# Copies of row sums moved from VectorE to GpSimd, and seven products in place of eight for one more block of tokens, in a fused attention and MLP kernel

## The chip, the cores and the metric

The kernel runs on one core of a Trainium2 chip. The core has five engines that each work through their own queue in order and meet by semaphores: TensorE (PE, matrix products), VectorE (DVE), ScalarE (ACT), GpSimd (POOL) and SyncE (SP, which here only issues DMAs). The metric is the device time of one execution in microseconds (us); lower is better.

## The reference

Attention over chunks of 64 keys, 8 batches, 8 heads, 576 rows, head size 64, and then a two-layer MLP with exact GELU on the 4608 tokens of 512 numbers that come out:

```
scores = (q_c @ k_c^T) / 8               # 64 x 64 blocks, one per batch, head and chunk
attn   = exp(scores - max); attn /= sum(attn) + 1e-9
x      = (attn @ v_c), heads side by side  # 4608 x 512
h      = x @ w_in                          # 512 x 2048
out    = (0.5 * h * (1 + erf(h / sqrt 2))) @ w_out
```

Inputs and outputs are float32. The kernel multiplies in bf16 and leaves out the subtraction of the maximum.

## The kernel before, in words

**Tiling.** The tokens are cut into nine tiles of 512, index t = 0 to 8. Tiles 0 to 7 hold the first eight chunks of one batch each, tile 8 the last chunk of all batches. A loop over t (L934) does for each index one *mm1* (x times w_in, GELU by ACT, result h) and one *mm2* (h times w_out, stored). Into the mm2 of index t, and into the mm1 of index t+1, the attention of a later tile is woven, so that PE always has something to do. The order of all engines is written out by hand: lists called `order`, `e1` (mm1) and `e2` (mm2) hold functions by step, and the place at which a function is called is the place of its instructions in each engine's queue. Nothing is reordered afterwards.

**mm1 with sixteen row blocks ("dense").** `mm1_slot` (L448) takes one block of 128 of the 2048 rows of h: four matmuls of 128x512, then one GELU (L455) out of one of three PSUM banks of the pool ps_mm. Indices in `DENSE` (L459) do this sixteen times.

**mm1 with seven products.** The other indices replace row blocks 0 to 3 by a 2x2 scheme with seven products instead of eight (`seven_rows` L508, `mm1_seven` L549): steps p1 to p7 are products of four 128x256 matmuls each (L523), built from sums of quarters of x (`x_sums` L502, four VectorE subtractions at L506) and of w_in. Three PSUM banks a, b, d collect them. ACT copies p1, p5 and u2 out (L527), VectorE adds a bank to such a copy (L530, steps c11, c12 and c22+), ACT applies GELU (L534). Step p3 is added into bank a, and so has to wait until the VectorE step c22+ has read bank a. Twelve row blocks remain dense.

**mm2 with seven products** (`mm2_seven` L604, matmuls at L664) needs sums of h. `g_sum` forms them on VectorE: sum 3 (L589, one instruction of 2048 columns), and sums 1, 2 and 4 in two halves each (L602, 1024 columns). The third product of mm2 reads both halves of sum 2. VectorE adds banks to copies at L631 and `store_block` lets SP issue the stores.

**The attention of tile n = t+1 from index 4 on.** In the mm2 of index t: scores of tile n+1 on PE (`quad_S` L231, 64 matmuls at L237, in four PSUM banks), exponentials on ACT (L244), and partial row sums on VectorE (`quad_part` L248: a transpose L254 and a reduction L257, four times). In the mm1 of index t+1 follows `quad_total` (L260): the sums lie in quarters of 32 partitions, and eight VectorE copies of 32 partitions by 32 numbers (L268, a quarter to its neighbour quarter) bring the missing half of each sum across; then for each half a reduction (L272), a reciprocal (L274), copies across (L279), and `quad_rc` (L281, L283), which spreads the reciprocals over columns, one of four tiles rc at a time. At the head of the next mm2 PE forms the value products (`quad_av`, 64 matmuls at L317, in four banks), and VectorE multiplies each bank by its rc into the next x (`quad_x` L321, L324). The four banks of `quad_S` in the same mm2 are the banks of `quad_av`, so PE's second half of the scores waits until the third and fourth of these multiplications are done.

**Loads.** `bring_qk` and `load_v_rows` let SP issue loads of q, k and v, and GpSimd casts what has landed to bf16 (L164, L212). In the body of index t stand, in this order, `flip_qk` of t+2 (two DMA transposes on SP), and then `next_loads`: q and k of t+3, v of t+2, with GpSimd's casts. SP's queue is in order too: the stores of index t-1 stand before these.

Of the kernel before, what the change touches and what calls it, by code (L numbers as in the profile page):

```python
# [11 lines left out]
def kernel(  # L12
# [20 lines left out]
    G = H // 2  # L33
# [5 lines left out]
    NT = B + 1  # L39
# [21 lines left out]
    QD = P // G  # L61
# [40 lines left out]
    tiles = [dict() for _ in range(NT)]  # L102
# [145 lines left out]
    def quad_part(t, g2, c):  # L248

        st = tiles[t]  # L250
        if c == 1:
# [5 lines left out]
        nc.vector.tensor_reduce(st["part", g2][:, c, :, :, 0], pt[:].rearrange("p n e u -> p n u e"),  # L257
                                axis=mybir.AxisListType.X, op=mybir.AluOpType.add)

    def quad_total(t, halves=range(2)):  # L260

        part = [tiles[t]["part", g2] for g2 in range(2)]
        if 0 in halves:
            tiles[t]["across"] = [work.tile([P, NB], f32, tag="across", name="across", bufs=2) for _ in range(2)]
            for g2 in range(2):
                for s in range(G):
                    o = s ^ 1
                    DV(part[g2][QD * s:QD * (s + 1), :, :, :, 1], part[g2][QD * o:QD * (o + 1), :, :, :, 0])  # L268
        across = tiles[t]["across"]
        for g2 in halves:  # L270
            total, rb = (work.tile([P, 2, NB], f32, tag=nm, name=nm, bufs=2) for nm in ("total", "rb"))
            nc.vector.tensor_reduce(total[:], part[g2][:].rearrange("p c n u s -> p c (n u) s"),  # L272
                                    axis=mybir.AxisListType.X, op=mybir.AluOpType.add)
            nc.vector.reciprocal(rb[:], total[:])  # L274
            tiles[t]["rb", g2] = rb[:, 0], across[g2][:]
            if g2 == 0:
                quad_rc(t, 0, 0)
            for r in range(2):
                DV(across[g2][CH * r:CH * (r + 1)], rb[CH * (1 - r):CH * (2 - r), 1])  # L279
# [176 lines left out]

    NQ = 4
    T0 = 3
    DENSE = (0, 1, T0 + 1)  # L459

    HF = FF // 2
    HD = d_model // 2
# [86 lines left out]
    def mm1_seven(t, hooks):  # L549

        tiles[t]["h"] = hpool.tile([P, FF, MT], bf16, tag="h", name="h")
        does = seven_rows(t, 0, {"a": AT, "b": AT, "d": AT}, AC)
        if t == NT - 1:
            sums = stage_tile()[:].bitcast(bf16).rearrange("p (i ks f) -> p i ks f", ks=2, f=HD)
            w_in_sum.append([sums[:, i] for i in range(4)])
            does["w"] = lambda: w_in_sums(1)
            more = seven_rows(t, 1, {"a": TP, "b": TP, "d": AT}, DV)
            does.update((step + "'", do) for step, do in more.items())
            order = ("p1", "p2", "p5", "c11", "w", 8, "p6", 9, "p4", "p7", "c12", "c22+", 10, "c22", "p1'", "p2'", "p3", 11,
                     "c11'", "p5'", 12, "p6'", 13, "p4'", "p7'", "c12'", "c22+'", 14, "c22'", "p3'", 15, "g0", "s3")  # L560
        elif t > T0:
            order = ("p1", "p2", "p5", "c11", "t0", 4, "p6", 5, 6, "p4", "p7", "c12", "c22+", "t1", 7, "c22", 8, 9, "p3",
                     10, "s3", 11, 12, 13, "g0", 14, 15)
        elif t == T0:
            order = ("x", "p1", "p2", 4, "p5", "c11", 5, "p6", 6, "p4", "p7", "c12", "c22+", 7, "c22", 8, "p3",
                     9, 10, "s3", 11, 12, 13, "g0", 14, 15)
        else:
            order = ("x", 4, 5, 6, "p1", "p2", 7, "p5", "c11", 8, "p6", 9, "p4", "p7", "c12", "c22+", 10, "c22", 11, "p3",
                     12, "s3", 13, "g0", 14, 15)
        for step in order:  # L570
            if step in does:
                does[step]()
                continue
            for u in hooks.get(step, ()):
                u()
            if not isinstance(step, str):
                mm1_slot(t, step)
# [230 lines left out]
    with tc.manual_schedule():  # L808
# [116 lines left out]
        def flip_qk(t):  # L925
            for nm in "qk":
                flip(t, nm)
# [6 lines left out]
        for t in range(1, NT):  # L934
# [3 lines left out]
            if t == 1:  # L938
# [12 lines left out]
                load_v_rows(2, (1,))  # L951
                cast_v_rows(2, PO)
                bring_qk(3)
            elif t > T0 and n + 1 < NT:
                flip_qk(n + 1)
            def next_loads():
                if t + 3 < NT:
                    bring_qk(t + 3)
# [39 lines left out]
                    e2[12] = parts[0]  # L998
                    e2[13] = parts[1]
            elif n < NT:  # L1000
                rcs = [lambda m=m: quad_rc(n, m // 2, m % 2) for m in range(1, G)]
                if t not in DENSE:
                    e1["t0"] = [lambda: quad_total(n, (0,))]
                    e1["t1"] = [lambda: quad_total(n, (1,))] + rcs
                else:
                    e1[1] = [lambda: quad_total(n)]
                    e1[5] = rcs
                e2 = {0: [exp, lambda: quad_av(n, ALONE)] + xs[:2] + g[1][:2], 4: xs[2:] + g[1][2:],
                      6: [lambda: x_sums(n, (0, 1))], 10: [lambda: x_sums(n, (2, 3))], 11: [gelu]}
                if n + 1 < NT:  # L1010
                    for i, gs in enumerate(((0,), (1, 2), (3,))):
                        e2.setdefault(2 * i + 2, []).append(lambda gs=gs: k_by_chunk(n + 1, AC, gs))
                    e2[8] = [lambda: quad_S(n + 1, ALONE)] + parts[0]
                    e2[10] += parts[1]
# [29 lines left out]
```

## Time and profile before

| | us |
|---|---|
| median of 3 runs (275.07 to 275.83) | 275.24 |
| the profiled execution, its own time | 277.53 |
| span of the profile, first to last instruction | 275.7 |
| PE busy | 265.3 (96%) |
| VectorE busy | 206.9 (75%) |
| ACT busy | 192.2 (70%) |
| GpSimd busy | 85.4 (31%) |
| mean granted clock of PE | 0.993 |

Times in a profile count from the start of the span. In the timeline a row gives start, length, engine, line of the kernel, operation, tiles and how many instructions were merged; square brackets give idle time of the engine just before, and what ended it. In a table of stages each row gives a stretch of the span and how long each engine was busy in it. By the starts of PE's steps, mm1 of index 4 begins at 137.66 us, its mm2 at 151.47; mm1 of index 5 at 165.22, its mm2 at 178.63; mm1 of index 6 at 192.44, its mm2 at 205.86; mm1 of index 7 at 219.60.

### The profile page before, as it was taken

Reading aid. Unit: us, or ns where it says so; the run is one execution under the profiler, and the core shown is the slowest. Engines: PE = TensorE matmul, PEld = TensorE weight load, DVE = VectorE, ACT = ScalarE, POOL = GpSimd, SP = SyncE. Lnnn points to the kernel's source line nnn. Section 1 sums busy time; section 2 is a strip of 40 time slices with the busy share of each in tenths; the row PEclk is TensorE's granted clock in tenths of the full one; section 3 lists DMA queues with packets and bytes.
Section 4 is the critical chain, followed back from the end, with each engine's and each line's share of the span. In section 5 each row is a group of like instructions: output and inputs, shape, how many; then the busy total and the mean of one; then the engine's idle time right before and its main releaser. Section 6 shows DMA issues by size and latency. Waiting matters only on the chain.

```text
span 275.7 us, 7136 instructions
## 1 busy us (share of the span) xinstructions
PE 265.3 (96%) x2863; PEld 182.0 (66%) x2885; DVE 206.9 (75%) x377; ACT 192.2 (70%) x368; POOL 85.4 (31%) x142
## 2 busy tenths in 40 slices
PE   8798999999999999999999999999999999999993
PEld 6473455445886588558844886588558855886683
DVE  5779425896893988587899789878987898746831
ACT  2765666987867877877966967896689778358610
POOL 7779668401176226104405800032300200000000
PEclk9979999999999999999999999999999999999999
DMA  6999999769899899999599517999974120130014
GB/s 221 254 360 402 394 388 239 189 157 277 263 376 204 220 326 188 263 273 302 141 248 344 132 40 195 160 132 162 242 169 108 66 76 2 40 105 9 4 38 114
DMA packets 104737, 53.94 MB, mean 196 GB/s; under 512 B 72960, under 2 KB 101632, under 8 KB 104704
## 3 DMA queue, kind: packets, MB, share of 16 engines
q1 hardware_dynamic: 104400, 53.23, 73.9%
q8 instruction: 22, 0.36, 0.5%
q10 hardware_dynamic: 304, 0.26, 0.3%
q14 instruction: 11, 0.09, 0.1%
HBM read 36.70 MB, written 9.44 MB: 167 GB/s over the span
## 4 chain that ended last, share of the span: by engine, by line
PE 91%; ACT 4%; DVE 2%; issue 1%; ACTq 0%
PE y_ps L664 34%; PE h_ps L453 34%; PE hs_ps L523 8%; PE y_ps L736 3%; PE av_ps L317 2%; ACT k_bd L188 2%; PE h_ps L443 2%; PE s_ps L237 1%; PE y_ps L700 1%; PE rc_ps L395 1%; PE tp L175 1%; PE none L800 1%; PE warm L794 1%; ACT pT L336 1%; PE av_ps L408 1%
## 5 line engine op out<-in xcount | busy, mean ns | idle before, releaser
L453 PE MATMUL h_ps<-x,w_in_sb 128*128 128x512 bf16 x420 | 98.0, 379 | 2.2 <-DVE w_in_sb L780 1.3
L455 ACT ACTIVATE h<-h_ps 128x512 bf16<-128x512 f32 x109 | 64.3, 597 | 21.5 <-PE h_ps L453 21.2
L453 PEld LDWEIGHTS <-w_in_sb 128*128 128x128 bf16 x436 | 42.5, 98 | 46.2 <-DVE w_in_sb L780 1.8
L664 PEld LDWEIGHTS <-h 128*128 128x128 bf16 x384 | 37.0, 98 | 4.7
L164 POOL CAST q_nat<-arrival 128x512 bf16<-128x512 f32 x31 | 20.4, 698 | 62.2 <-DMA arrival<-in_q_dram 58.3
L212 POOL CAST v_nat<-arrival 128x1024 bf16<-128x1024 f32 x14 | 15.0, 1078 | 49.3 <-DMA arrival<-in_v_dram 49.3
L664 PE MATMUL y_ps<-v_bd,k_bd 128*128 128x256 bf16 x256 | 29.4, 273 | 0.1
L664 PE MATMUL y_ps<-w_out_sb,h 128*128 128x256 bf16 x256 | 29.3, 273 | 0.0
L664 PEld LDWEIGHTS <-k_bd 128*128 128x128 bf16 x256 | 24.8, 98 | 3.2 <-DVE w_out_sb L500 0.2
L631 DVE TENSOR_TENSOR kept<-y_ps,kept 128x512 f32<-128x512 f32 (+1 forms) x25 | 16.4, 656 | 12.3 <-PE y_ps L664 8.7
L806 ACT ACT_TABLE_LOAD x18 | 23.1, 1283 | 1.0 <-PEq L1028 0.7
L626 ACT COPY kept<-y_ps 128x512 f32<-128x512 f32 (+1 forms) x26 | 14.5, 556 | 12.3 <-PE y_ps L664 12.1
L164 POOL CAST k_nat<-arrival 128x512 bf16<-128x512 f32 x30 | 18.9, 666 | 11.8 <-DMA arrival<-in_v_dram 6.1
L530 DVE TENSOR_TENSOR arrival<-hs_ps,arrival 128x512 f32<-128x512 f32 x21 | 13.8, 685 | 11.2 <-PE hs_ps L523 7.2
L534 ACT ACTIVATE h<-arrival 128x512 bf16<-128x512 f32 x21 | 13.2, 628 | 6.6 <-DVE arrival L530 6.4
L664 PE MATMUL y_ps<-v_bd,s_sb 128*128 128x256 bf16 x128 | 15.3, 273 | 0.0
L664 PE MATMUL y_ps<-w_out_sb,s 128*128 128x256 bf16 x128 | 15.3, 273 | 0.0
L664 PE MATMUL y_ps<-v_bd,h 128*128 128x256 bf16 x128 | 15.3, 273 | 0.0
L244 ACT ACTIVATE pT<-s_ps 128x512 bf16<-128x512 f32 x28 | 14.4, 603 | 0.1
L602 DVE TENSOR_TENSOR k_bd<-h 128x1024 bf16<-128x1024 bf16 x16 | 11.1, 696 | 3.6 <-ACT h L455 3.4
L664 PEld LDWEIGHTS <-s 128*128 128x128 bf16 x128 | 12.4, 98 | 1.5
L636 ACT COPY y_sb<-y_ps 128x512 f32<-128x512 f32 x7 | 4.1, 586 | 13.2 <-PE y_ps L664 13.2
(130 smaller groups left out, 428.1 us busy)
## 6 DMA issues: line engine op xcount, KB each, us to landing
arrival<-in_v_dram SPq DMA_DIRECT2D x58, 128.0 KB, 4.0
arrival<-in_q_dram SPq DMA_DIRECT2D x7, 1024.0 KB, 6.5
arrival<-in_k_dram SPq DMA_DIRECT2D x6, 1024.0 KB, 9.3
out_dram<-kept SPq DMA_DIRECT2D x21, 256.0 KB, 2.7
arrival<-in_moe_w_out_dram SPq DMA_DIRECT2D x4, 1024.0 KB, 11.2
arrival<-in_moe_w_in_dram SPq DMA_DIRECT2D x6, 512.0 KB, 6.6
out_dram<-y_sb SPq DMA_DIRECT2D x11, 256.0 KB, 2.5
arrival<-in_k_dram SPq DMA_DIRECT2D x8, 256.0 KB, 5.3
```

Source lines behind the costliest of these rows:

```text
L164: copy(st[nm][:, g].rearrange("p j r d -> p r j d"), st[nm + "f"][:, 2 * g:2 * g + 2])
L212: copy(st["v"][:, r::2], st["vf"][:, r::2])
L244: nc.scalar.activation(pT[:].rearrange("p u (c j) -> p u c j", j=J), s_ps[g2][c][:].rearrange("p u (j c) -> p u c j", j=J), Act.Exp, scale ...
L453: nc.tensor.matmul(h_ps[:], w_in_sb[:, ks, f * P:(f + 1) * P], tiles[t]["x"][:, ks, :], start=(ks == 0), stop=(ks == KS - 1))
L455: nc.scalar.activation(tiles[t]["h"][:, f, :], h_ps[:], Act.Gelu)
L523: nc.tensor.matmul(bank[to][:, f], left[:, ks, f * P:(f + 1) * P], right[:, ks], start=(fresh and f == 0 and ks == 0), stop=(ks == 1), ski ...
L530: nc.vector.tensor_tensor(home[name], bank[src][:], home[name], op=ADD)
L534: nc.scalar.activation(h[:, n:n + HM, HD * c:HD * (c + 1)], src, Act.Gelu)
L626: nc.scalar.copy(kept[name][:, ms], ps[:])
L631: nc.vector.tensor_tensor(y_sb[:, ms], ps[:], y_sb[:, ms], op=ADD)
L664: nc.tensor.matmul(to, left(f, m), right[:, f], start=(fresh and (split or m == 0) and f == 0), stop=(f == HF - 1), skip_group_check=True)
L806: nc.scalar.activation(act_scratch[:], rest[:, 0:1], func)
```

## The change

Three things change, all from index 4 on. The eight copies of partial row sums become a function of their own, `quad_across`, on GpSimd (`PO`) instead of VectorE (`DV`); it is called at the head of the body of indices 4 to 7, ahead of the DMA transposes and of the casts of that index. Of the four spreads `quad_rc`, two (the third and fourth) move out of mm1 into step 2 of mm2. And index 4 leaves `DENSE`: its mm1 has twelve dense row blocks and the seven products, in an order of its own, with all four `x_sums` at its head; in its mm2 the second halves of sums 1 and 2 now stand ahead of the first two multiplications (L324).

```diff
@@ -257,15 +257,19 @@
         nc.vector.tensor_reduce(st["part", g2][:, c, :, :, 0], pt[:].rearrange("p n e u -> p n u e"),
                                 axis=mybir.AxisListType.X, op=mybir.AluOpType.add)
 
+    def quad_across(t):
+
+        part = [tiles[t]["part", g2] for g2 in range(2)]
+        for g2 in range(2):
+            for s in range(G):
+                o = s ^ 1
+                PO(part[g2][QD * s:QD * (s + 1), :, :, :, 1], part[g2][QD * o:QD * (o + 1), :, :, :, 0])
+
     def quad_total(t, halves=range(2)):
 
         part = [tiles[t]["part", g2] for g2 in range(2)]
         if 0 in halves:
             tiles[t]["across"] = [work.tile([P, NB], f32, tag="across", name="across", bufs=2) for _ in range(2)]
-            for g2 in range(2):
-                for s in range(G):
-                    o = s ^ 1
-                    DV(part[g2][QD * s:QD * (s + 1), :, :, :, 1], part[g2][QD * o:QD * (o + 1), :, :, :, 0])
         across = tiles[t]["across"]
         for g2 in halves:
             total, rb = (work.tile([P, 2, NB], f32, tag=nm, name=nm, bufs=2) for nm in ("total", "rb"))
@@ -456,7 +460,7 @@
 
     NQ = 4
     T0 = 3
-    DENSE = (0, 1, T0 + 1)
+    DENSE = (0, 1)
 
     HF = FF // 2
     HD = d_model // 2
@@ -558,6 +562,9 @@
             does.update((step + "'", do) for step, do in more.items())
             order = ("p1", "p2", "p5", "c11", "w", 8, "p6", 9, "p4", "p7", "c12", "c22+", 10, "c22", "p1'", "p2'", "p3", 11,
                      "c11'", "p5'", 12, "p6'", 13, "p4'", "p7'", "c12'", "c22+'", 14, "c22'", "p3'", 15, "g0", "s3")
+        elif t == T0 + 1:
+            order = ("x", 4, 5, 6, 7, "p1", "p2", 8, "p5", "c11", "t0", 9, "p6", 10, "p4", "p7", "c12", "c22+", "t1",
+                     11, "c22", 12, 13, "p3", "s3", 14, "g0", 15)
         elif t > T0:
             order = ("p1", "p2", "p5", "c11", "t0", 4, "p6", 5, 6, "p4", "p7", "c12", "c22+", "t1", 7, "c22", 8, 9, "p3",
                      10, "s3", 11, 12, 13, "g0", 14, 15)
@@ -951,8 +958,10 @@
                 load_v_rows(2, (1,))
                 cast_v_rows(2, PO)
                 bring_qk(3)
-            elif t > T0 and n + 1 < NT:
-                flip_qk(n + 1)
+            if t > T0 and n < NT:
+                quad_across(n)
+                if n + 1 < NT:
+                    flip_qk(n + 1)
             def next_loads():
                 if t + 3 < NT:
                     bring_qk(t + 3)
@@ -998,15 +1007,15 @@
                     e2[12] = parts[0]
                     e2[13] = parts[1]
             elif n < NT:
-                rcs = [lambda m=m: quad_rc(n, m // 2, m % 2) for m in range(1, G)]
-                if t not in DENSE:
-                    e1["t0"] = [lambda: quad_total(n, (0,))]
-                    e1["t1"] = [lambda: quad_total(n, (1,))] + rcs
-                else:
-                    e1[1] = [lambda: quad_total(n)]
-                    e1[5] = rcs
-                e2 = {0: [exp, lambda: quad_av(n, ALONE)] + xs[:2] + g[1][:2], 4: xs[2:] + g[1][2:],
+                rcs = [lambda m=m: quad_rc(n, m // 2, m % 2) for m in range(G)]
+                if t == T0 + 1:
+                    e1["x"] = [lambda: x_sums(t)]
+                e1["t0"] = [lambda: quad_total(n, (0,))]
+                e1["t1"] = [lambda: quad_total(n, (1,)), rcs[1]]
+                e2 = {0: [exp, lambda: quad_av(n, ALONE)] + xs[:2] + g[1][:2], 2: rcs[2:], 4: xs[2:] + g[1][2:],
                       6: [lambda: x_sums(n, (0, 1))], 10: [lambda: x_sums(n, (2, 3))], 11: [gelu]}
+                if t == T0 + 1:
+                    e2[0] = e2[0][:2] + g[1][:2] + xs[:2]
                 if n + 1 < NT:
                     for i, gs in enumerate(((0,), (1, 2), (3,))):
                         e2.setdefault(2 * i + 2, []).append(lambda gs=gs: k_by_chunk(n + 1, AC, gs))
```

## The prediction

> **What bounds the kernel now.** I read the page's busy times first, then the chain of waits, then a table of stages that are one mm1 or one mm2 long, and last the timelines of PE, VectorE and GpSimd in indices 4 to 6.
>
> ```profile
> PE 265.3 (96%) x2863; PEld 182.0 (66%) x2885; DVE 206.9 (75%) x377; ACT 192.2 (70%) x368; POOL 85.4 (31%) x142
> ...
> PE 91%; ACT 4%; DVE 2%; issue 1%; ACTq 0%
> ```
> ```profile
> 137.66:151.47 13.81, 13.71 (x70) 6.11 (x74) 13.08 (x31) 9.54 (x16) 3.45 (x4) 1.00 1.05 293
> 151.47:165.22 13.75, 13.75 (x242) 12.20 (x243) 11.07 (x21) 11.21 (x16) 5.78 (x7) 1.00 0.35 90
> 165.22:178.63 13.41, 13.30 (x82) 7.26 (x86) 12.17 (x30) 10.42 (x19) 0.00 (x0) 1.00 0.92 176
> ...
> 192.44:205.86 13.42, 13.31 (x82) 7.24 (x86) 12.73 (x30) 10.25 (x19) 2.90 (x4) 1.00 0.88 214
> ...
> sum 95.36, PE 94.94 PEld 64.53 DVE 82.61 ACT 74.23 POOL 18.16; mean PE 13.56 PEld 9.22 DVE 11.80 ACT 10.60 POOL 2.59
> ```
>
> The rows of stages give length, then busy time of PE, its weight loads, VectorE, ACT and GpSimd. The first is mm1 of index 4 (dense), the third that of index 5 (seven products). Over indices 4 to 7, up to 233.02, PE idles 95.36 - 94.94 = 0.42 us in all, at the full granted clock (1.00). So a change here can gain only by giving PE less work, and loses whenever it makes PE wait. VectorE is next, 12 to 13 us in an mm1 of 13.4: what PE needs from it has little lead.
>
> ```profile
> 148.02 4.03 POOL L164 CAST q_nat<-arrival 128x512 bf16<-128x512 f32 x4 [11.84 <-DMA arrival<-in_q_dram]
> 152.00 3.28 POOL L164 CAST k_nat<-arrival 128x512 bf16<-128x512 f32 x4
> 155.23 2.02 POOL L212 CAST v_nat<-arrival 128x1024 bf16<-128x1024 f32 x2
> 182.57 2.30 POOL L164 CAST q_nat<-arrival 128x512 bf16<-128x512 f32 x4 [25.32 <-DMA arrival<-in_q_dram]
> 191.01 2.29 POOL L164 CAST k_nat<-arrival 128x512 bf16<-128x512 f32 x4 [6.15 <-DMA arrival<-in_v_dram]
> 193.25 1.05 POOL L212 CAST v_nat<-arrival 128x1024 bf16<-128x1024 f32 x1
> 197.13 1.05 POOL L212 CAST v_nat<-arrival 128x1024 bf16<-128x1024 f32 x1 [2.84 <-DMA arrival<-in_v_dram]
> ```
> ```profile
> 153.83 0.98 DVE L602 TENSOR_TENSOR k_bd<-k_bd,h 128x1024 bf16<-128x1024 bf16 x1
> ...
> 155.83 0.69 DVE L631 TENSOR_TENSOR kept<-y_ps,kept 128x512 f32<-128x512 f32 x1 [1.02 <-PE y_ps L664]
> ...
> 180.98 0.69 DVE L602 TENSOR_TENSOR k_bd<-k_bd,h 128x1024 bf16<-128x1024 bf16 x1
> ...
> 182.99 0.69 DVE L631 TENSOR_TENSOR kept<-y_ps,kept 128x512 f32<-128x512 f32 x1 [1.32 <-PE y_ps L664]
> ...
> 194.42 1.51 DVE L268 COPY part<-part 32x32 f32<-32x32 f32 x8
> ...
> 198.42 1.29 DVE L530 TENSOR_TENSOR arrival<-hs_ps,arrival 128x512 f32<-128x512 f32 x2
> ```
>
> To be seen here: GpSimd's casts end with transfers, and the last one for v of tile 7 starts 4.69 us into index 6 (197.13 - 192.44), later than VectorE's copies of the row sums stand now (194.42). And one subtraction takes 0.69 us alone but 0.98 while casts run, which then take 1.0 instead of 0.57.
>
> **Index 4's mm1: less work on PE.** Sixteen blocks take 13.81 us; twelve with seven products take 13.41 in index 5. Gain **0.40**. ACT goes from 9.54 to about 10.4 busy, as in index 5, and fits. VectorE gets four subtractions at L506 (1.7 by their spacing in index 4's mm2) and three additions at L530 (0.68 each), and loses eight copies (1.51) and two spreads (1.24).
>
> **Index 4: sums of h come later.** Sum 3 (L589) needs the GELU of p3. In the new order ten blocks (13.81/16 = 0.863) and seven products (0.437, from the chain's 0.87 for eight matmuls) end with p3 at 137.66 + 8.63 + 3.06 = 149.35; ACT is then busy with block 13 till 149.5 and needs 0.6: sum 3 starts at 150.1, where it started at 147.34. From there VectorE needs, by index 5's rows, 3.48 for sum 3 and the first halves (174.58 to 178.06) and 1.40 for two second halves (180.27 to 181.67), with gaps: 155.1 at the earliest. GpSimd casts k and v in just this stretch. Rows of index 4 show casts and subtractions taking turns, a pair in 1.02; so four subtractions with k casts 4.1, and the fifth with a v cast about 1.5: 150.1 + 1.2 + 4.1 + 1.5 = **156.9**. I take this, since q's casts start at 148.02 by a transfer that nothing here moves, and k's follow. PE wants the last half (mm2's third product, fifth matmul) at 137.66 + 13.41 + 0.67 + 3.50 + 0.44 = 155.7 and waits 1.2.
>
> Behind it VectorE has the first two multiplications (1.21), the two moved spreads (1.24), L631 (0.61), and the other two multiplications (1.29): with a gap of 0.1, to 161.3 (159.5 without casts). PE reaches the second half of the scores at 151.07 + 0.67 + 7.0 + 0.33 = 159.1, and their banks are those of these multiplications. In all PE loses **2.2** in this mm2 (bounds 0.4 and 3.0, the latter if both v casts hold up a subtraction). Before, the multiplications ended at 157.73 and PE came at 159.2: nothing waited.
>
> [...]
>
> **VectorE stays late into index 5.** From the fourth multiplication's end to the last L631 of index 4 VectorE has 157.73 to 166.63, less 0.99 idle: 7.9 us without a pause, while PE needs 0.35 + 5.26 to index 5. So that L631 ends 2.3 after the start of index 5, not 1.41: **0.9** later. SP's store of it, and behind it in SP's queue the transposes and the loads of q and k of tile 8 and v of tile 7, move with it: from that L631 to the last v cast 30.5 us passed (166.63 to 197.13), DMA busy at a share of 0.92 and more. SP's queue itself is not reordered.
>
> **Index 6: the copies queue behind a transfer.** On GpSimd the copies for tile 7 stand after both v casts of tile 7. Those end 4.69 + 1.05 + 0.9 = 6.6 us into index 6. A copy of 32 columns: casts of 512 follow each other in 0.56, of 1024 in 0.98, so 0.14 fixed and 0.03 for 32 columns, 0.17 (between 0.11, the 64x16 memset, and 0.29, the 128x128 cast). The first half's total needs four: 7.4 with a semaphore. VectorE waits there in order, and behind it stand c12 and c22+: reduction, reciprocal, spread and copies take 1.74 (168.80 to 170.54), the two L530 1.29: c22+ ends at 10.45. PE wants p3 at 200.24, that is 7.8 in: a wait of 2.65. ACT's GELU for c12 waits likewise with evictions of blocks 7 to 9 behind it, at 0.5 each; block 11 then waits another 0.3 for a bank. Together **3.0** (bounds 1.5 without the 0.9 and with copies of 0.11; 3.6 with copies of 0.29).
>
> **What costs nothing.** Copies in index 4 (sums ready at 141.2, GpSimd idle from 136.19 to 148.02), in index 5 (ready at 166.03 + 0.9, idle from 157.25 to 182.57) and in index 7 (v casts over at 215.66). If GpSimd were busy there, each would cost like index 6. The moved spreads in indices 5 to 7: 1.24 us into VectorE's idle 1.32 before L631 (182.99). The 1.5 us that VectorE saves per mm1 in 5 and 7 gains nothing, for PE did not wait.
>
> **Sum.** -0.40 + 2.2 + 3.0 = +4.8. The profiled execution (span 275.7, own time 277.53, so 1.8 around the span) would become 280.5 and 282.3. The median of runs, 275.24, lies 2.3 below that execution; with the same addition it becomes **280.0**.
>
> **Rivals.**
> 1. Both waits, as above: 280.0, chance 0.57.
> 2. Index 4 stays within its bound of 0.4, because casts fall between subtractions: 275.24 - 0.40 + 0.4 + 3.0 = 278.2. For it: the second half of sum 1, at 153.10, ran in 0.69 although a cast started with it. Chance 0.13.
> 3. The v rows of tile 7 land 3 us earlier, and only index 4 pays: 277.0. Against it: the transfers run at full share from 171.76 on. Chance 0.10.
> 4. Every subtraction is blocked for a whole cast: 4 x 0.62 + 1.04 = 3.5 on 155.1, the multiplications end at 163.0, PE loses 3.9: 281.7. Chance 0.08. [...]
> 5. Not slower: without the profiler the transfers are so much faster that GpSimd is always ahead. It decides when the casts of index 4 are over by 150.1 (7 us earlier than 157.25) and the last v cast of index 6 starts by 2.9 (1.8 earlier). Then 275.24 - 0.40 + 0.4 = 275.2, or 274.8 with index 4's bound gone too. For it: the profiled execution was 2.3 us longer. Against it: that is under 1% of all. Chance 0.12, of which 0.04 for something faster than 274.4, for which PE's idle 0.42 has no room.
>
> **How the numbers follow.** About 0.3%, 0.8 us, is what a measurement here can tell from no change. Rivals 1 to 4 are slower: 0.88; within 0.3%: 0.08; faster: 0.04. The range from 276.8 to 281.8 holds rivals 1 to 4 with their bounds.
>
> **What would show it.** In the changed kernel's profile: mm1 of index 4 in 13.4; PE's gaps in index 4's mm2 at the third product and at the scores, released by VectorE; in index 6 GpSimd's copies directly after the last v cast, some 5 us of VectorE idle before the reduction, released by POOL, and a PE gap before p3, released by VectorE's addition. I am wrong if GpSimd's copies run before VectorE asks for them in index 6, or if casts and sums do not meet in index 4.

## The result, and the profile after

The changed kernel takes **278.88 us** (median of 6 runs, 277.87 to 280.09), the kernel before beside it 275.18 (6 runs, 274.83 to 275.85). The ratio is 1.0132, with a 95% interval from 1.0098 to 1.0166: slower, by 3.7 us. The forecast was 280.0 with a range from 276.8 to 281.8. Medians in this text are of all runs, and ratios leave out runs more than 1.5% above the fastest of their kernel, of which only two kernels below have any: the held casts with a new tile (the two runs that count average 288.86) and the tile of 64 bytes (283.90).

The profiled execution took 280.0 us, its span is 278.0. Two lines of its page, the busy times and the chain of work that ended last:

```profile
PE 265.9 (96%) x2875; PEld 183.3 (66%) x2897; DVE 206.7 (74%) x352; ACT 193.3 (70%) x371; POOL 94.4 (34%) x174
...
PE 74%; DVE 9%; DMA 6%; SPq 4%; ACT 3%; issue 2%; POOL 1%; ACTq 0%; DVEq 0%; POOLq 0%
```

TensorE's share of busy time says nothing here (96% before and after). The chain shows where to look: before, 91% of it was PE, and now VectorE, transfers and SP's queue have taken 17 points of it. Those points are not time lost. In index 5 the chain runs back through a load and SP's queue while PE works on undisturbed.

Where the time lies is read from the table of stages: time from the first PE instruction of a step to the first of the next, then busy time of PE, its weight loads, VectorE, ACT and GpSimd, PE's clock, the share of the DMA engines and GB/s. The rows are mm1 and mm2 of index 4, then of 5, then of 6.

```profile
136.23:149.74 13.51, 13.40 (x76) 7.35 (x76) 10.94 (x25) 10.41 (x19) 5.00 (x14) 1.00 1.04 292
149.74:166.16 16.42, 14.37 (x241) 12.21 (x241) 15.94 (x26) 11.26 (x16) 8.03 (x10) 1.00 0.32 82
166.16:179.67 13.51, 13.40 (x76) 7.33 (x75) 9.84 (x20) 10.53 (x19) 0.83 (x4) 1.00 0.90 176
179.67:193.33 13.66, 13.66 (x242) 12.10 (x242) 12.34 (x21) 11.21 (x16) 4.51 (x7) 1.00 1.11 159
193.33:207.90 14.57, 13.82 (x78) 7.33 (x77) 10.20 (x21) 10.09 (x19) 4.50 (x12) 1.00 0.82 190
207.90:221.71 13.81, 13.81 (x241) 12.10 (x241) 12.87 (x22) 11.21 (x16) 3.39 (x6) 1.00 0.33 87
```

Cut at the same instructions, the kernel before has 13.91, 13.65, 13.51, 13.72, 13.51 and 13.65. So mm1 of index 4 became 0.40 shorter, its mm2 2.77 longer (16.42 - 13.65), and mm1 of index 6 1.06 longer (14.57 - 13.51); the rest adds 0.1. From the start of index 4 to the end of the span the changed kernel takes 278.0 - 136.23 = 141.8 us, the one before 275.7 - 137.49 = 138.2: 3.6 more, close to the 3.7 of the medians. In the slowed mm2 VectorE is busy for 15.94 of 16.42 us, and the granted clock is 1.00, so PE is made to wait and is not throttled.

PE's timeline in that mm2 and in index 6 (start, duration, engine and line, operation, tiles; in brackets the idle time before the row and what ended it):

```profile
153.91 0.60 PE L671 MATMUL y_ps<-v_bd,k_bd 128*128 128x256 bf16 x4
155.82 3.23 PE L671 MATMUL y_ps<-v_bd,k_bd 128*128 128x256 bf16 x28 [1.31 <-DVE k_bd L609]
158.99 0.74 PE L237 MATMUL s_ps<-q_t,k_c 64*64 64x64 bf16 x34
160.02 0.44 PE L237 MATMUL s_ps<-q_t,k_c 64*64 64x64 bf16 x30 [0.29 <-DVE x L328]
160.39 1.92 PE L671 MATMUL y_ps<-v_bd,s_sb 128*128 128x256 bf16 x16
162.15 1.91 PE L671 MATMUL y_ps<-w_out_sb,s 128*128 128x256 bf16 x16
164.42 1.91 PE L671 MATMUL y_ps<-v_bd,h 128*128 128x256 bf16 x16 [0.37 <-DVE kept L638]
...
201.93 0.60 PE L527 MATMUL hs_ps<-k_bd,w_in_sb 128*128 128x256 bf16 x4 [0.64 <-DVE arrival L534]
```

In the kernel before, the same products and scores, p3 of index 6, and last a VectorE addition that is used further down:

```profile
155.57 3.66 PE L664 MATMUL y_ps<-v_bd,k_bd 128*128 128x256 bf16 x32
159.16 0.71 PE L237 MATMUL s_ps<-q_t,k_c 64*64 64x64 bf16 x64
159.80 1.92 PE L664 MATMUL y_ps<-v_bd,s_sb 128*128 128x256 bf16 x16
163.30 1.91 PE L664 MATMUL y_ps<-v_bd,h 128*128 128x256 bf16 x16
200.08 0.60 PE L523 MATMUL hs_ps<-k_bd,w_in_sb 128*128 128x256 bf16 x4
...
165.95 0.68 DVE L631 TENSOR_TENSOR kept<-y_ps,kept 128x512 f32<-128x512 f32 x1
```

There are three gaps in index 4 and one in index 6, all released by VectorE; before there was none. Start to start they cost more than the brackets say. Undisturbed, one of mm2's matmuls follows the other in 0.109 us (32 in 3.50), so the third product loses 155.82 - 153.91 - 4 x 0.109 = 1.47, the scores take 160.39 - 158.99 = 1.40 where they took 0.64 before (159.80 - 159.16), and the last product loses 164.42 - 162.15 - 1.75 = 0.52. Together 2.75. The third gap, before `y_ps<-v_bd,h`, stands nowhere in the forecast.

VectorE and GpSimd beside it, index 4 first:

```profile
148.80 1.46 DVE L596 TENSOR_TENSOR s_sb<-h 128x2048 bf16<-128x2048 bf16 x1 [1.16 <-ACT h L538]
150.19 1.09 DVE L609 TENSOR_TENSOR k_bd<-h 128x1024 bf16<-128x1024 bf16 x1
...
154.36 1.41 DVE L609 TENSOR_TENSOR k_bd<-k_bd,h 128x1024 bf16<-128x1024 bf16 x1
...
163.69 0.68 DVE L638 TENSOR_TENSOR kept<-y_ps,kept 128x512 f32<-128x512 f32 x1
...
198.84 0.22 DVE L276 TENSOR_REDUCE total<-part 128x32 f32<-128x64 f32 x1 [2.93 <-POOL part L266]
...
200.59 1.29 DVE L534 TENSOR_TENSOR arrival<-hs_ps,arrival 128x512 f32<-128x512 f32 x2
```
```profile
149.51 4.27 POOL L164 CAST k_nat<-arrival 128x512 bf16<-128x512 f32 x4 [0.32 <-DMA arrival<-in_k_dram]
153.74 2.93 POOL L212 CAST v_nat<-arrival 128x1024 bf16<-128x1024 f32 x2
...
196.76 1.04 POOL L212 CAST v_nat<-arrival 128x1024 bf16<-128x1024 f32 x1 [1.61 <-DMA arrival<-in_v_dram]
197.86 1.96 POOL L266 COPY part<-part 32x32 f32<-32x32 f32 x8
```

In index 4 the subtractions run from 148.80 to 155.77, k's casts start 0.7 us later and v's end at 156.67: the two series lie on one another, each subtraction takes 0.9 to 1.4 us and each of k's casts 1.07. In index 6 GpSimd waits 1.61 us for v's transfer, casts it, and only then comes to the copies; VectorE stands idle for 2.93 us before the reduction that needs four of them, and its addition at 200.59 is the one that PE waits for at 201.93.

### The profile page after: what moved, and what is told of

Read it like the earlier page. It is cut to its first block, busy times and chain, and to the rows that moved or that the text cites. A ratio compares the mean times of both kernels' runs of the same rounds, so it can differ in the third digit from the quotient of the medians.

```text
span 278.0 us, 7180 instructions
## 1 busy us (share of the span) xinstructions
PE 265.9 (96%) x2875; PEld 183.3 (66%) x2897; DVE 206.7 (74%) x352; ACT 193.3 (70%) x371; POOL 94.4 (34%) x174
## 4 chain that ended last, share of the span: by engine, by line
PE 74%; DVE 9%; DMA 6%; SPq 4%; ACT 3%; issue 2%; POOL 1%; ACTq 0%; DVEq 0%; POOLq 0%
PE h_ps L457 26%; PE y_ps L671 26%; PE hs_ps L527 7%; PE y_ps L743 3%; DMA arrival<-in_k_dram 3%; DMA arrival<-in_q_dram 2%; PE h_ps L447 2%; SPq L194 1%; DMA arrival<-in_v_dram 1%; PE tp L175 1%; SPq L128 1%; PE y_ps L707 1%; PE av_ps L321 1%; PE rc_ps L399 1%; DVE k_bd L609 1%
## 5 line engine op out<-in xcount | busy, mean ns | idle before, releaser
L457 PE MATMUL h_ps<-x,w_in_sb 128*128 128x512 bf16 x404 | 95.3, 379 | 0.8
L459 ACT ACTIVATE h<-h_ps 128x512 bf16<-128x512 f32 x105 | 62.0, 596 | 18.2 <-PE h_ps L457 17.6
L457 PEld LDWEIGHTS <-w_in_sb 128*128 128x128 bf16 x420 | 41.0, 98 | 42.0 <-issue 0.3
L164 POOL CAST q_nat<-arrival 128x512 bf16<-128x512 f32 x31 | 19.1, 654 | 48.2 <-DMA arrival<-in_q_dram 30.6
L212 POOL CAST v_nat<-arrival 128x1024 bf16<-128x1024 f32 x14 | 16.1, 1160 | 45.0 <-DMA arrival<-in_v_dram 44.8
L534 DVE TENSOR_TENSOR arrival<-hs_ps,arrival 128x512 f32<-128x512 f32 x24 | 15.8, 685 | 13.7 <-PE hs_ps L527 9.8
L164 POOL CAST k_nat<-arrival 128x512 bf16<-128x512 f32 x30 | 20.1, 703 | 12.0 <-DMA arrival<-in_k_dram 7.3
L638 DVE TENSOR_TENSOR kept<-y_ps,kept 128x512 f32<-128x512 f32 (+1 forms) x25 | 16.4, 655 | 7.6 <-PE y_ps L671 3.7
L538 ACT ACTIVATE h<-arrival 128x512 bf16<-128x512 f32 x24 | 15.1, 627 | 8.0 <-DVE arrival L534 8.0
L609 DVE TENSOR_TENSOR k_bd<-h 128x1024 bf16<-128x1024 bf16 x16 | 11.8, 736 | 3.7 <-ACT h L459 3.7
L527 PEld LDWEIGHTS <-w_out_sb 128*128 128x128 bf16 x112 | 11.0, 98 | 4.9
```

What stands on the lines that cost most here:

```text
L164: copy(st[nm][:, g].rearrange("p j r d -> p r j d"), st[nm + "f"][:, 2 * g:2 * g + 2])
L212: copy(st["v"][:, r::2], st["vf"][:, r::2])
L457: nc.tensor.matmul(h_ps[:], w_in_sb[:, ks, f * P:(f + 1) * P], tiles[t]["x"][:, ks, :], start=(ks == 0), stop=(ks == KS - 1))
L459: nc.scalar.activation(tiles[t]["h"][:, f, :], h_ps[:], Act.Gelu)
L527: nc.tensor.matmul(bank[to][:, f], left[:, ks, f * P:(f + 1) * P], right[:, ks], start=(fresh and f == 0 and ks == 0), stop=(ks == 1), ski ...
L534: nc.vector.tensor_tensor(home[name], bank[src][:], home[name], op=ADD)
```

## The experiments

Theory A is the prediction's account: in index 4 the late sums meet the casts, and in index 6 the copies queue on GpSimd behind a cast that waits for a transfer. The expectations name the other theories beside it.

**Each part alone.** The first kernel is the one before with nothing changed but the copies.

```diff
 (in the kernel before)
-            for g2 in range(2):
-                for s in range(G):
-                    o = s ^ 1
-                    DV(part[g2][...], part[g2][...])
...
-            elif t > T0 and n + 1 < NT:
-                flip_qk(n + 1)
+            if t > T0 and n < NT:
+                quad_across(n)          # the same copies, with PO
+                if n + 1 < NT:
+                    flip_qk(n + 1)
```

> The kernel before with one part of the change: the copies of the row sums on GpSimd from index 4 on; index 4 stays dense and no spread moves. Two theories. A (two separate waits): the copies cost only in index 6, where they stand behind the cast of v of tile 7; the profile of the changed kernel had 1.1 us there, the cast's own start differs by up to 1.4 us between profiles, so +0.6 to +2.4 us, about 276.3, and no PE gap in index 4's mm2. B (the copies are hidden everywhere and all of the loss is index 4's): 275.2 and no PE gap before p3 of index 6.

Measured: 276.93 us (12 runs, 275.66 to 278.69), ratio 1.0064 (1.0039 to 1.0088). Index 4 stays at 13.65 for mm2; mm1 of index 6 takes 15.60, 2.09 more than undisturbed. Its PE, GpSimd and VectorE rows in index 6, which begins at 190.34:

```profile
199.99 0.60 PE L527 MATMUL hs_ps<-k_bd,w_in_sb 128*128 128x256 bf16 x4 [1.68 <-DVE arrival L534]
```
```profile
194.80 1.04 POOL L212 CAST v_nat<-arrival 128x1024 bf16<-128x1024 f32 x1 [2.38 <-DMA arrival<-in_v_dram]
195.91 1.96 POOL L266 COPY part<-part 32x32 f32<-32x32 f32 x8
```
```profile
196.89 0.22 DVE L276 TENSOR_REDUCE total<-part 128x32 f32<-128x64 f32 x1 [4.37 <-POOL part L266]
```

Theory B, in which index 6 costs nothing, is out. It is the same order of events as in the changed kernel, only later against PE: here the last cast starts 4.46 into index 6, there 3.43, and the loss is 2.09 against 1.06. The differences are the same, 1.03.

The second is the changed kernel with the copies back on VectorE, where they stood; the spreads and the seven products stay.

```diff
-            if t > T0 and n < NT:
-                quad_across(n)
-                if n + 1 < NT:
-                    flip_qk(n + 1)
+            elif t > T0 and n + 1 < NT:
+                flip_qk(n + 1)
... and the eight DV copies again in quad_total
```

> The changed kernel with the copies back on VectorE, in their old place; the seven products of index 4 and the two moved spreads stay. A: PE loses 2.7 us in index 4's mm2 and gains 0.4 in its mm1, so +2.3 to +2.6 us, about 277.6, and index 6 costs nothing. [...]

Measured: 277.84 us (6 runs, 277.22 to 278.46), ratio 1.009 (1.0062 to 1.0119). mm2 of index 4 takes 16.56, index 6 13.61: the whole of index 4's loss without the copies, and next to nothing of index 6's. PE in index 4:

```profile
154.57 3.23 PE L667 MATMUL y_ps<-v_bd,k_bd 128*128 128x256 bf16 x28 [1.45 <-DVE k_bd L605]
...
158.76 0.44 PE L237 MATMUL s_ps<-q_t,k_c 64*64 64x64 bf16 x30 [0.29 <-DVE x L324]
...
163.16 1.91 PE L667 MATMUL y_ps<-v_bd,h 128*128 128x256 bf16 x16 [0.36 <-DVE kept L634]
```

The three gaps are those of the changed kernel, so the copies do not cause them. The two parts add up to (276.93 - 275.17) + (277.84 - 275.17) = 4.4, against 3.7 for both together. The intervals of the three ratios are wide enough for that difference; in the profiles index 6 differs by more (2.09 against 1.06), where the loss depends on when v lands (below).

**Index 6: take the transfer from ahead of the copies.** In the changed kernel tile 7's casts of v go behind its copies in GpSimd's order.

```diff
                 quad_across(n)
+                if n == 7:
+                    cast_v_rows(n, PO)
...
                     load_v_rows(n + 1)
-                    cast_v_rows(n + 1, PO)
+                    if n + 1 != 7:
+                        cast_v_rows(n + 1, PO)
```

> The changed kernel with one move in GpSimd's queue: the two casts of v of tile 7 stand behind the copies for tile 7. A: the wait in index 6 goes (1.1 us in the profile), 277.8, the copies run 0.5 us after the partial sums, and the single runs lie closer together than the 2.2 us of the changed kernel, since no transfer is left in PE's way. D (the copies themselves are too slow, 0.24 us each): the wait shrinks by under 0.3 us, 278.6.

Measured: 277.89 us (6 runs, 277.27 to 278.5), ratio 1.009 (1.0059 to 1.012). mm1 of index 6, which begins at 192.69, is back at 13.51:

```profile
190.94 2.60 POOL L164 CAST k_nat<-arrival 128x512 bf16<-128x512 f32 x4 [3.69 <-DMA arrival<-in_v_dram]
193.60 1.97 POOL L266 COPY part<-part 32x32 f32<-32x32 f32 x8
195.64 2.02 POOL L212 CAST v_nat<-arrival 128x1024 bf16<-128x1024 f32 x2
```

The copies take as long as before and VectorE still needs four of them; they only start 0.91 into index 6. So it was the place in GpSimd's queue, not the price of a copy (theory D). The run times alone would not carry this: the intervals of this ratio and of the changed kernel's overlap, and in this profile index 4's third product loses less too, 0.84 instead of 1.47, with q's casts starting later (148.37 against 146.91) and so meeting other sums. The runs also spread less than those of the changed kernel (1.2 us against 2.2), but the kernel before spreads by 2.3 over 17 runs, so nothing is read from that.

The cure holds when it is given to all tiles: the kernel of the first experiment with the casts of v for tiles 6 to 8 behind the copies.

```diff
                 quad_across(n)
+                if t > T0 + 1:
+                    cast_v_rows(n, PO)
...
-                    cast_v_rows(n + 1, PO)
+                    if t <= T0:
+                        cast_v_rows(n + 1, PO)
```

> x1 (the kernel before with the copies alone on GpSimd) with the v casts of tiles 6 to 8 behind the copies. A (x1's 1.8 us are the wait behind the transfer of v): no wait is left and nothing is gained either, 275.2, within 0.3%. D (the copies themselves cost on GpSimd): 276 to 277.

Measured: 275.01 us (12 runs, 274.64 to 275.66), ratio 0.9974 (0.9956 to 0.9992), and mm1 of index 6 takes 13.51. The two kernels' runs, 12 each, do not overlap but for one value (275.66 is the slowest here and the fastest there). So copies on GpSimd as such cost nothing that shows, the interval lying even a little below 1; in the first experiment their whole price was the wait behind the transfer.

**Index 4: take the casts away from the sums.** In the changed kernel the casts of index 4 are held until VectorE has done the second half of sum 2; a small GpSimd operation that reads this sum holds them.

```diff
+                    def held_casts():
+                        PO(hold_scratch[:], flat(k_bds[3], 1)[:, 0, 0:1])
+                        pool_cast_qk(t + 3)
+                        cast_v_rows(n + 1, PO)
-                    e2[0] = e2[0][:2] + g[1][:2] + xs[:2]
+                    e2[0] = e2[0][:2] + g[1][:2] + [held_casts] + xs[:2]
... the two casts are left out of next_loads at index 4;
+    hold_scratch = consts.tile([P, 1], bf16, name="hold_scratch")
```

> The changed kernel with GpSimd's casts of q, k of tile 7 and v of tile 6 held in index 4 until VectorE has written the second half of sum 2 (a GpSimd copy of one column of that sum stands before them; it adds one small instruction). A: the casts made VectorE's sums late; without them the second half of sum 2 comes 1.8 us earlier and PE's gaps in index 4's mm2 fall from 2.7 to between 0.4 and 0.9 us, 276.8. E (the sums are late only because p3's GELU is late, the casts do not matter): under 0.4 us gained, 278.6.

Measured: 291.27 us (6 runs, 286.79 to 293.66), ratio 1.049 (1.0415 to 1.0566): far from every expectation. In the stage that the experiment is about, sums and scores ran without a gap, as theory A says, but a new one came up, and index 4's mm2 takes 18.28. That is only half of the loss: the profile's span is 9.2 us longer than before (284.9 against 275.7), of which 4.6 lie in this mm2, 3.0 ahead of index 4 (it begins at 140.46 against 137.49) and 2.05 in mm1 of index 6, less the 0.40 gained in mm1 of index 4. Nothing that the experiment was meant to change lies ahead of index 4, but its new tile stands ahead of other tiles in the order of allocation. To test whether that is the reason, only the new tile was left out, and the small operation's result was written to an old one:

```diff
-    hold_scratch = consts.tile([P, 1], bf16, name="hold_scratch")
...
-                        PO(hold_scratch[:], flat(k_bds[3], 1)[:, 0, 0:1])
+                        PO(ident_f[:, 0:1], flat(k_bds[3], 1)[:, 0, 0:1])
```

> As x4_hold_casts (index 4's casts held until the second half of sum 2), but the holding instruction writes into a tile that the kernel already has, so that nothing else in SBUF moves. In the profile of x4 the waits at sum 2 and at the scores were gone, and the held casts then kept one half of sum 4 waiting for 2.5 us, which PE paid with 0.5 + 2.5 us; but the whole kernel took 291. G (the new two-byte tile, which moves every tile behind it, made the rest slow): 278.9 to 279.9 here, as index 4 loses 3.0 in place of 2.7 us and the transfers are as before. H (holding the casts by itself makes the loads late and the kernel slow): again above 285.

Measured: 279.87 us (4 runs, 279.81 to 280.17), ratio 1.015 (1.0126 to 1.0175). A tile of two bytes per partition had cost 9 us (288.86 against 279.87); the runs of the last section follow this up. In this kernel's index 4 VectorE, GpSimd and PE show:

```profile
147.57 1.23 DVE L596 TENSOR_TENSOR s_sb<-h 128x2048 bf16<-128x2048 bf16 x1 [1.16 <-ACT h L538]
...
151.56 0.69 DVE L609 TENSOR_TENSOR k_bd<-k_bd,h 128x1024 bf16<-128x1024 bf16 x1
...
156.39 3.17 DVE L609 TENSOR_TENSOR s<-h,k_bd 128x1024 bf16<-128x1024 bf16 x1
```
```profile
152.51 2.29 POOL L164 CAST q_nat<-arrival 128x512 bf16<-128x512 f32 x4
154.75 2.29 POOL L164 CAST k_nat<-arrival 128x512 bf16<-128x512 f32 x4
156.99 2.02 POOL L212 CAST v_nat<-arrival 128x1024 bf16<-128x1024 f32 x2
```
```profile
159.62 1.48 PE L671 MATMUL y_ps<-w_out_sb,s 128*128 128x256 bf16 x12 [0.34 <-DVE s L609]
163.44 2.90 PE L671 MATMUL y_ps<-v_bd,h 128*128 128x256 bf16 x16 [2.35 <-DVE kept L638]
```

Without casts the sums take from 147.57 to 152.25, 4.68 us instead of 6.97, and PE waits neither at the third product nor at the scores. So the casts cost VectorE 2.3 us in the changed kernel, and without them both of those gaps (2.2) are gone. Sum 3 starts as late as in the changed kernel (12.57 into index 4 in both), so that lateness alone costs PE nothing. The new gap is the price of moving the casts: one subtraction, at 156.39, met casts that followed each other without a break, and took 3.17 us instead of 0.69, ending 0.55 behind the last of them (159.56 against 159.01). Behind it in VectorE's queue stands the L638 that the last product needs, and PE waits 2.35 us for it. More is lost than the wait: this mm2 takes 17.63, 3.98 above 13.65. The two gaps are 0.51 and 2.51 start to start, and the other 0.95 is PE's clock: the 16 matmuls behind the long gap take 2.90 us instead of 1.91. In the 4.56 us behind the long gap (163.44 to 168.00) the granted clock is 0.63 instead of 1.00 (the page has 0.7 for 160.0 to 167.0), which also lengthens mm1 of index 5 by 0.72, to 14.23.

In the changed kernel both grew where they met: a subtraction took 0.9 to 1.4 us and one of k's casts 1.07, as in turns. Here only the subtraction did: k's four casts took 2.29 and v's two 2.02, as in rows of the kernel before (2.29 at 191.01, 2.02 at 155.23). In the kernel with the new tile the same subtraction, at 161.83, took 3.17 us as well and ended 0.54 behind the last cast. What decides between the two courses was not tried.

**The moved spreads.** In the changed kernel index 4's two spreads go back into mm1; the other indices keep them in mm2.

```diff
-                e1["t1"] = [lambda: quad_total(n, (1,)), rcs[1]]
+                e1["t1"] = [lambda: quad_total(n, (1,)), rcs[1]] + (rcs[2:] if t == T0 + 1 else [])
-                ... 2: rcs[2:], ...
+                ... 2: rcs[2:] if t > T0 + 1 else [], ...
```

> The changed kernel with the two moved spreads of index 4 back in its mm1, where VectorE idled 1.2 us before sum 3. A (every instruction that VectorE has between the sums and the last multiplication delays PE): the wait for sum 2 stays near 1.5, the waits at the scores (0.75) and at the last product (0.5) go, so 1.0 to 1.3 us less, 277.7. F (only the sums are late, the moved spreads are free as they are in indices 5 to 7): under 0.3 us less, 278.7.

Measured: 277.39 us (12 runs, 276.33 to 278.59), ratio 1.0072 (1.0049 to 1.0095): 1.5 less than the changed kernel. mm2 of index 4 takes 15.25 instead of 16.42. PE:

```profile
154.00 3.23 PE L671 MATMUL y_ps<-v_bd,k_bd 128*128 128x256 bf16 x28 [1.32 <-DVE k_bd L609]
157.16 0.71 PE L237 MATMUL s_ps<-q_t,k_c 64*64 64x64 bf16 x64
...
161.42 1.91 PE L671 MATMUL y_ps<-v_bd,h 128*128 128x256 bf16 x16
```

The gap at the third product stays, since nothing ahead of it has moved. The gap at the scores (0.76) is gone, and of that at the last product (0.52) 0.11 is left (161.42 - 159.56 - 1.75): together 1.17 us less, for 1.24 us of spreads taken out of VectorE's queue. So the unforeseen third gap has the same cause as the second: after the scores VectorE never had a pause in which to catch up. And the gap at the scores needs both causes, since it goes without the casts as well as without the spreads.

**The changes that the gaps point to, together.** The changed kernel with v's casts behind the copies for tiles 6 to 8, index 4's spreads in mm1, both halves of sum 4 behind the second pair of multiplications, and the four `x_sums` for the next index together at step 10 of mm2.

```diff
                 quad_across(n)
+                if t > T0 + 1:
+                    cast_v_rows(n, PO)
...
                 if t == T0 + 1:
+                    e1["g0"] = g[0][:2]
                     e2[0] = e2[0][:2] + g[1][:2] + xs[:2]
+                    e2[4] = xs[2:] + [g[0][2], g[1][2]]
+                    e2[6] = []
+                    e2[10] = [lambda: x_sums(n)]
... and the spreads as above
```

> A version that should beat both: the changed kernel with the v casts of tiles 6 to 8 behind the copies on GpSimd, and in index 4 the spreads back in mm1, both halves of sum 4 behind the multiplications, and all four sums of x behind the first addition at L638. A: the second half of sum 2 comes 1.0 us earlier, all three waits of index 4 and the one of index 6 are gone or under 0.3 us, and the 0.4 us of PE's work show: 274.8 to 275.4. If other waits take their place: 276 or more.

Measured: 274.63 us (12 runs, 274.07 to 277.69), ratio 0.9984 (0.9958 to 1.001). Its stages (mm1 and mm2 of index 4, mm1 of index 6):

```profile
134.88:148.39 13.51, 13.41 (x76) 7.32 (x75) 12.09 (x27) 10.42 (x19) 4.70 (x13) 1.00 1.03 290
148.39:162.06 13.67, 13.67 (x242) 12.05 (x241) 13.21 (x22) 11.21 (x16) 5.22 (x8) 1.00 0.39 99
189.22:202.73 13.51, 13.40 (x76) 7.32 (x76) 11.22 (x20) 10.44 (x19) 4.76 (x12) 1.00 0.90 196
```

All gaps are gone and the gain of 0.40 in mm1 of index 4 is left, so this version is 4.2 us faster than the changed kernel. Against the kernel before it shows no difference that these runs can tell, nor against the copies alone (275.01): 0.40 of 275 is 0.15%.

## Why the prediction was right, and where its sizes were off

- **Index 4's mm1, -0.40**: 13.91 became 13.51. Right.
- **Index 4's sums, 2.2 at the third product and the scores**: 1.47 and 0.76. The steps hold one by one: sum 3 starts 12.57 into index 4 (predicted 150.1 - 137.66 = 12.4), the second half of sum 2 ends 19.5 in (19.2), the fourth multiplication ends 23.7 in (161.3 - 137.66 = 23.6), and the casts of k and v lie on the sums (from 13.3 to 20.4 in), as the sum needed. The held casts show the cause, with the gaps of 2.2 going away; the spreads, which the forecast also counted between sums and scores, are the other condition of the gap at the scores.
- **What was missed in index 4, 0.52**: the last product waits for L638 of the bank it writes. The forecast followed who is late next as far as the scores, and then followed VectorE's lateness to the next index. But between those lies another bank that VectorE empties, and PE waits there.
- **"VectorE stays late into index 5", 0.9**: did not come. The last L638 of index 4 ends 167.11 + 0.68 - 166.16 = 1.63 into index 5, against 1.58 before, both counted from the first `hs` matmul. Most of it was the same lateness, paid by PE: once PE had waited 0.52 at the last product as well, index 5 began that much later, and what was left to be late was 0.05. Another part was never there: the forecast's 2.3 counts from the first `hs` matmul, its 1.41 from a start 0.17 later.
- **Index 6, 3.0**: measured 1.06. The mechanism is the one predicted, to the engine and the row, and the chain that ended last runs as it was drawn, from a store behind index 4 through SP's queue and the loads to v's cast (168.28 to 196.76); the term is mis-sized. The last cast of v ends 197.80 - 193.33 = 4.5 into index 6 instead of 6.6: 0.9 is the lateness that was not there, the other 1.2 is the transfer, which landed earlier than in the profile before. Against that it is 1.04 from the cast's end to the reduction (197.80 to 198.84) instead of 0.8, since the copies follow each other in 0.24, not 0.17. The chain behind it took 3.04 as predicted (198.84 to 201.88). VectorE's idle time before the reduction was 2.93 accordingly, not some 5.
- **What costs nothing**: copies in indices 4, 5 and 7, spreads in 5 to 7. Right: mm1 of indices 4, 5 and 7 takes 13.51 in the changed kernel, mm2 of 5 and 6 13.66 and 13.81 (13.72 and 13.65 before).
- **Sum**: -0.40 + 2.2 + 0.5 + 1.1, with 0.1 of rest, is 3.5, for +4.8 foreseen: an excess of 1.9 in index 6 and a lack of 0.5 in index 4. That the total came within 1.2 us is partly luck: the two errors have opposite signs, and the term of index 6 came out anywhere from 0 to 2.1 in kernels of much the same time, with the landing of v (table below). Of the rivals, that of a whole cast for each subtraction is out in this kernel (index 4 lost 2.75, not 3.9), and that of free turns too (0.4). No run shows the first one's term, a whole cast of 0.62 for each subtraction: beside casts of k one took 0.22 to 0.40 us more than its 0.69 here, and with the casts held a single one took 2.48 more. The rival in which only index 4 pays (277.0) is what the third experiment made of it (277.89). The range does not hold the rivals with all their bounds, as was said: with index 4 at 0.4 rival 3 gives 275.2, and with index 6 at 3.6 rival 4 gives 282.3.

Index 6's term has a sharp form. In the profiles of the kernels that have tile 7's casts ahead of its copies on GpSimd, the loss of mm1 of index 6 (its length less 13.51) goes with the start of v's last cast, counted from the first matmul of index 6:

| kernel | last cast starts | loss | start less 2.37 |
|---|---|---|---|
| copies only (before + copies) | 4.46 | 2.09 | 2.09 |
| held casts with the new tile | 4.41 | 2.05 | 2.04 |
| changed, two bytes at the end | 4.03 | 1.65 | 1.66 |
| changed, spreads back | 3.59 | 1.23 | 1.22 |
| changed | 3.43 | 1.06 | 1.06 |
| held casts without the tile | 3.01 | 0.65 | 0.64 |
| changed, 512 bytes | 2.09 | 0.00 | -0.28 |
| changed, 64 bytes among the constants | 5.75 | 4.50 | 3.38 |
| changed, two bytes among the constants | 6.22 | 5.40 | 3.85 |

(The four with bytes are in the last section.) From 3.0 to 4.5 all that the transfer is late is lost by PE in full. The kernel before has this cast at 4.85 (197.13 - 192.28) and loses nothing, since its copies do not stand behind it. The last two rows lie outside and lost more. PE's only wait there is again the one for VectorE's addition, of 2.96 and 3.44 us, but behind it the granted clock falls: in the last row it is 0.60 from 209.75 to 214.00 (the page has 0.7 for 208.2 to 215.4). The prediction put the point from which it costs at 2.9; the rows give 2.37, half of the difference by dearer copies (0.24) and half because another 0.25 is lost behind the wait at p3. The last casts of v start 2 us apart in profiles of two kernels that differ from the changed one only by an unused tile that cost nothing (2.09 and 4.03). So a good part of what this change costs may be drawn anew in each execution; that is not shown, as each kernel has one profile. Why v lands earlier in one than in another stays open.

## What to carry to other kernels

An operation moved to an engine that is mostly idle also takes a place in that engine's queue. Ask what stands ahead of it there and what that waits for: here eight copies of 0.2 us cost 2 us behind a cast that waited for a transfer, and nothing ahead of it. Follow lateness on one engine through all the places where another waits for it, and count it once: what one engine has waited is no longer late. Before two engines' work is put on the same stretch, look whether their rows grow when they overlap, in the profile of before.

## What was not expected of the hardware

**Two bytes ahead of the other tiles cost 4% of the time** (290.19 us against 278.88). The held casts with a new two-byte tile took 286.8 to 293.7 us, without it 279.8 to 280.2. To see whether it is the tile, the changed kernel got an unused one, written once by GpSimd, of two and of 64 bytes per partition:

```diff
     act_scratch = consts.tile([P, 1], f32, name="act_scratch")
+    spare = consts.tile([P, 1], bf16, name="spare")      # or [P, 32]
...
         act_table(Act.Exp)
+        nc.gpsimd.memset(spare[:], 0.0)
```

> The changed kernel with one unused tile of two bytes per partition added among the constants, written once. Theory G (the place in SBUF of the tiles behind it makes the transfers longer): some 290 us, as with the held casts and the new tile (291.3 against 279.9 without it); the transfers' share of 16 engines' span above 75%, and mm1 of index 4 starting some 5 us later than at 136.23. The rival (the held casts themselves, or that run, were slow for another reason): the changed kernel's 278.9, share 72 to 74%.

> The same with a tile of 64 bytes per partition in its place. Theory G: 278 to 280 us, the changed kernel's 278.9, because the tiles behind it keep their place modulo 64 bytes. A rival of G, that any added tile costs it (whatever its size): as with two bytes, some 290.

Measured: two bytes 290.19 us (4 runs, 289.0 to 291.1), ratio 1.0543 (1.0506 to 1.0581); 64 bytes 286.29 (4 runs, 283.29 to 290.59), ratio 1.0317 (1.0275 to 1.0359). Even the fastest of these is above every run of the changed kernel (280.09 at most), so 64 bytes cost as well, and theory G with its modulus of 64 fell. Two more runs separate the place from the tile and from its one instruction: 512 bytes in the same place (`consts.tile([P, 256], bf16, ...)`), and two bytes in a pool allocated behind all other tiles.

> The changed kernel with an unused tile of 512 bytes per partition among the constants, a part of it written once by GpSimd. Theory H (where the tiles behind it begin, counted modulo some power of two up to 512 bytes, makes the transfers longer; 2 and 64 bytes shifted them, 512 do not): the changed kernel's 278.9, the transfers' share of 16 engines' span 72 to 74%. Rival I (any added tile ahead of the others, or the instruction that writes it, costs it): 284 to 290, share 75 to 76%.

> The changed kernel with the unused tile of two bytes in a pool of its own, allocated behind all other tiles, so that none of these moves; written once by GpSimd as before. Theory H: 278.9, since nothing is shifted. Rival I in the form that the writing instruction or the allocation itself costs: some 290, as with two bytes among the constants.

Measured: 512 bytes 278.25 us (9 runs, 277.58 to 279.31), ratio 1.01 (1.0069 to 1.0131); two bytes at the end 279.16 (4 runs, 278.24 to 279.68), ratio 1.0132 (1.0078 to 1.0186). Both are the changed kernel's time. So neither an added tile nor its instruction costs anything; 2 or 64 bytes ahead of the other tiles do, 512 do not. That these tiles begin that much later is taken from the order of allocation; their addresses were not read. The transfer queue's line of the page (packets, MB, share of 16 engines' span), with two bytes, with 512 bytes:

```profile
q1 hardware_dynamic: 104400, 53.23, 75.8%
```
```profile
q1 hardware_dynamic: 104400, 53.23, 73.7%
```

Same packets and bytes, but 0.758 x 287.2 = 217.7 us of transfer instead of 0.737 x 276.1 = 203.5: 7% more. The same product is 217.8 with 64 bytes and 216.8 for the held casts with the new tile, and between 201 and 205 in the kernels before and after, with the seven products alone, with the held casts without the tile, with the changes together, and with two bytes at the end. Index 4 starts at 141.91 instead of 135.37, PE having waited before it, 2.89 us at once, for sums whose work had come late; v then lands late in index 6, too, whose mm1 takes 18.91. If a modulus decides, as theory H has it, 128, 256 and 512 all fit these runs, since 512 is a multiple of each and 64 of none; that one decides, and how a tile's place would lengthen transfers, is not shown.

**After a long wait PE's clock was not full for some us.** Behind waits of 2.35, 2.89, 2.96 and 3.44 us the granted clock fell to 0.5 to 0.7 for 3 to 5 us. On the pages it is 0.8 for 163.8 to 170.9 and 0.7 for 160.0 to 167.0 in the held casts with and without the tile (2.35 each), 0.7 for 129.2 to 136.4 and for 208.2 to 215.4 with two bytes (2.89, 3.44), and 0.7 for 207.5 to 214.7 with 64 bytes (2.96). Behind waits of up to 1.68 PE kept its pace (four matmuls took 0.60 us behind 1.68 in the copies alone, as elsewhere; behind 1.31 in the changed kernel the clock was 1.00), but also behind one of 2.72 (64 bytes, 131.89 to 136.00, where the page has 0.9 or more), so these runs give no length from which it happens.

**A small copy on GpSimd** of 32x32 f32 follows the next in 0.24 us, so eight take 1.96; on VectorE eight took 1.51. And **one subtraction beside casts without a break** took 3.17 us instead of 0.69 in both kernels with held casts, while k's four casts took their usual 2.29; in the changed kernel, where they also met, it was 0.9 to 1.4 for a subtraction and 1.07 for one of k's casts.
